# Token blocks of 384 instead of 256 in a pooled-attention and rational-MLP kernel on one Trainium2 core

## The chip, the cores and the metric

The kernel runs on one core of one Trainium2 chip. The metric is the time of one execution on the device in microseconds (us), lower is better. The engines are named as in the profile: PE (TensorE, matmuls; PEld its weight loads), DVE (VectorE), ACT (ScalarE), POOL (GpSimd) and SP (SyncE, which here only issues DMAs). A ratio is time after over time before.

## The reference, cut to what matters

```python
# q, k, v: batch 8, heads 8, seq 576, head_dim 64, float32; pool = 8, so 72 pooled keys
k_p = k.reshape(B, H, 72, 8, D).mean(axis=3)
v_p = v.reshape(B, H, 72, 8, D).mean(axis=3)
scores = D ** -0.5 * q @ k_p.T
attn = softmax(scores) ; attn_out = attn @ v_p
x = attn_out.transpose(0, 2, 1, 3).reshape(4608, 512)     # tokens x d_model
h = x @ w_in                                              # 512 x 2048
P = a0 + a1*h + a2*h^2 + a3*h^3 ; Q = 1 + |b0|*|h| + |b1|*h^2
out = (P / (Q + 1e-6)) @ w_out                            # 2048 x 512, float32
```

## The kernel before

**Tiling.** The 4608 tokens are 18 blocks of `TOK` = 256, `d_ff` is `NU` = 8 units of 256 columns, and one step is one block with one unit. A step has three parts:

- `mm1`: h for 256 columns of `d_ff` by 256 tokens. x and `w_in` are each held as a high and a low part, and three products are summed (high x high, low weight x high, high weight x low): for each of two halves of 128 columns, 3 x 4 matmuls with 256 columns, so 24 into one PSUM bank, tile `ph`.
- `rational` with `quotient`: P/Q of a 128 x 512 tile, in 6 ACT, 5 DVE and 2 POOL instructions (tiles `w`, `r`, `t`, and `rp` in PSUM); the result is split again into `gh` and `gl`.
- `mm2`: 12 matmuls with 512 columns, six for each half of 128 tokens, into two banks `po`, which stay open over all units of a block and are then evicted (`evict`) and stored. The first two blocks are an exception: they run units 0 to 3 first, their x and their partial sums go out to DRAM (`spill`, `parts`), and units 4 to 7 come later (`reload`), so that the weights have time to arrive.

**Attention** (`attend`) makes x of a block. `squares` loads q; `attention` makes, for each tile of 128 tokens, q turned (`qT`), the scores (`ps`), the softmax (tile `e`) and turns that; for blocks from the fifth on q and the softmax are turned in 32 x 32 squares by DVE, and 16 DMAs a block bring the squares from `e` to their places in `am` (high part `hi`, low part `lo`). For the first four blocks PE does the turning (`pq`, `pm`, `pr`). `values` multiplies with the pooled v (tiles `pv`): 16 matmuls a block, or 32 where a batch ends inside the block, since batches have 576 tokens. Six of the 18 blocks have such an end inside. `prep_k` and `prep_v` pool k and v once a batch. The tiles `q`, `am0`, `am1` and `e` have one buffer each, the x tiles `x0` and `x1` two buffers each.

**What sets the order.** Nothing is issued directly. Every call adds an `Op` to a `Plan` with an engine, a cost and a due time (`due(at)`, spaced `SLOW` or `PACE` us a step; single ones are moved by the table `LATER`, which goes by the number of the op). `Plan.solve` then lays the ops out engine by engine by due time, with the pools' buffers as a constraint, and `Plan.issue` emits them in that order, so all instructions carry the one line L309. The PSUM pool `ps` has 8 buffers, one bank each, for `ph`, `rp`, `po`, `ps`, `pv` and the transposes. Where the plan leaves PE free, `issue` puts in matmuls of no use (line L301), which keep PE occupied: into the tile `idle` at the start, and from the first open `po` on, products with zero into an open sum:

```python
elif sums:
    to, one, first = list(sums.values())[-1][:, 0:256].ap(), self.zeros, False
...
while free is not None and to is not None:
    free += 0.12 if free > self.WARM else 0.215
    if free > op.start:
        break
    self.nc.tensor.matmul(to, lhsT=self.filler, rhs=one, start=first, stop=first)
```

Of the kernel before, what the change touches and what calls it, by code (L numbers as in the profile page):

```python
# [72 lines left out]
class Buf:  # L73


    def __init__(self, ring, shape, dtype, name):
        self.ring, self.shape, self.dtype, self.name = ring, shape, dtype, name
        self.writes, self.reads, self.left, self.held, self.it = [], [], 0, False, None
        self.slot, self.users = None, []

# [7 lines left out]
class Ring:  # L88


    def __init__(self, pool, tag, bufs, loose):
        self.pool, self.tag, self.loose = pool, tag, loose
        self.free, self.queue = [(0.0, i) for i in range(bufs)], []


class Op:
    __slots__ = ("eng", "cost", "port", "calls", "deps", "users", "bufs", "due", "wait",
                 "ready", "seq", "bytes", "early", "slack", "start", "end", "done", "lead")


class Plan:
# [3 lines left out]
    HOP = {"sp": 0.035, "pe": 0.035, "pool": 0.08, "dve": 0.035, "act": 0.035}  # L105
# [22 lines left out]
    def __init__(self, nc):  # L128
        self.nc, self.ops, self.rings, self.now, self.slack = nc, [], {}, 0.0, 1.9

# [9 lines left out]
    def add(self, eng, cost, calls, port=False, claims=(), bytes=0, early=34.0, after=()):  # L140
        op = Op()
        op.eng, op.cost, op.port, op.calls, op.bytes = eng, cost, port, calls, bytes
        op.early, op.slack, op.lead = early, self.slack, 0.0
        op.seq, op.due, op.deps, op.users = len(self.ops), self.now, set(), []
# [38 lines left out]
    def solve(self):  # L183
# [17 lines left out]
        while done < len(self.ops):  # L201
            best = None
            for e, cands in engs.items():
                pick = None
                opts = []
                for op in cands:
# [13 lines left out]
                    else:  # L220
                        for r, n in need.values():
                            mine = [b for b in op.bufs if not b.held and b.ring is r]
                            if len(r.free) < n or not r.loose and any(
# [104 lines left out]
def tile_pooled_attention_then_rational_moe(  # L328
# [20 lines left out]
    P = 128  # L349
# [307 lines left out]
    def squares(i):  # L657
# [4 lines left out]
        if i < 4:  # L662
            return qs
# [358 lines left out]
```

## Time and profile before

| | |
|---|---|
| time, median of 3 runs | 899.14 us (899.04 to 899.77) |
| the profiled execution's own time | 898.87 us |
| its span in the profile | 897.2 us |
| granted clock of PE, mean | 0.995 |
| PE busy | 881.1 us, 98% |
| DVE, ACT, POOL busy | 753.1 (84%), 683.2 (76%), 521.3 (58%) |

The profiled execution's time has 1.67 us around the span, and lies 0.27 us under the median of the runs. A matmul's row shows some 275 to 385 ns from its start to its end, but matmuls follow each other much closer, so what one costs is read from the starts of its neighbours in the timeline, not from the mean of its group. In the same way ACT's and DVE's instructions overlap by about 0.1 us.

### The profile page before, as it was taken

What the parts mean: (1) busy time and instruction counts of PE and PEld (TensorE: products, weight loads), DVE (VectorE), ACT (ScalarE), POOL (GpSimd) and SP (SyncE); (2) the same over time, 40 slices, a digit from 0 to 9 for tenths busy, and PEclk for the clock granted to TensorE, in tenths of its full rate; (3) what the DMA queues carried; (4) which work ended last, traced back from release to release, by engine and by line L of the source; (5) the groups of instructions that cost most, each with busy time, mean ns of one, the idle gap of its engine ahead of it and who ended that gap; (6) DMA issues with size and microseconds to landing.
All of it is one profiled execution on the core that took longest, in us unless ns stands there. A gap on an engine that the chain in (4) does not pass through costs nothing.

```text
span 897.2 us, 17205 instructions
## 1 busy us (share of the span) xinstructions
PE 881.1 (98%) x6124; PEld 823.8 (92%) x6124; DVE 753.1 (84%) x1337; ACT 683.2 (76%) x1124; POOL 521.3 (58%) x472
## 2 busy tenths in 40 slices
PE   8799999999999999999999999999999999999998
PEld 8798999899988999999999899999999999999997
DVE  6889997998979869988889699789898977988664
ACT  3799899887676769686877787497868684968774
POOL 5777678886446545455736483467546754545444
PEclk9999999999999999999999999999999999999999
DMA  9996111145133412122613251134222422202000
GB/s 304 300 380 212 32 48 47 51 117 134 44 87 94 107 24 60 30 60 52 131 28 72 54 123 39 31 77 119 59 39 51 96 58 34 51 1 59 2 24 23
DMA packets 185080, 75.31 MB, mean 84 GB/s; under 512 B 162340, under 2 KB 162340, under 8 KB 184996
## 3 DMA queue, kind: packets, MB, share of 16 engines
q1 hardware_dynamic: 184996, 74.23, 32.1%
q8 instruction: 48, 0.79, 0.4%
q14 instruction: 36, 0.29, 0.1%
HBM read 50.59 MB, written 12.58 MB: 70 GB/s over the span
## 4 chain that ended last, share of the span: by engine, by line
PE 81%; ACT 6%; SPq 4%; DMA 3%; DVE 2%; issue 2%; POOL 1%; POOLq 0%; ACTq 0%; DVEq 0%
PE po L309 36%; PE ph L309 36%; PE pv L309 4%; SPq L309 4%; PE ps L309 3%; DMA early<-in_v_dram 2%; ACT rp L309 1%; DVE t L309 1%; ACT r L309 1%; DVE m_wout L309 1%; ACT w L309 1%; ACT t L309 1%; POOL wout L309 1%; DMA ob<-pd 0%; ACT wout L309 0%
## 5 line engine op out<-in xcount | busy, mean ns | idle before, releaser
L309 PEld LDWEIGHTS ph<-x,win 128*128 128x128 f32 x3264 | 455.1, 191 | 32.0 <-issue 0.7
L309 PE MATMUL ph<-x,win 128*128 128x256 f32 x3264 | 464.7, 276 | 0.5 <-ACT x L309 0.4
L309 PE MATMUL po<-wout,gh 128*128 128x512 f32 x1152 | 333.5, 383 | 0.5 <-POOL wout L309 0.3
L309 POOL TENSOR_TENSOR w<-w,r 128x512 f32<-128x512 f32 (+1 forms) x145 | 188.4, 1300 | 216.7 <-ACT r L309 181.3
L309 POOL TENSOR_TENSOR gl<-t,gh 128x512 fp32r<-128x512 f32 (+1 forms) x145 | 189.4, 1307 | 84.3 <-ACT gh L309 70.1
L309 PEld LDWEIGHTS po<-wout,gh 128*128 128x128 f32 x1152 | 187.3, 191 | 10.6 <-ACT gh L309 0.9
L309 PE MATMUL po<-wout,gl 128*128 128x512 f32 x576 | 172.6, 382 | 0.1
L309 DVE SCALAR_TENSOR_TENSOR t<-t,abn,rp 128x512 f32<-128x512 f32 (+1 forms) x145 | 106.8, 736 | 67.2 <-ACT rp L309 65.6
L309 ACT ACTIVATE rp<-w,cbias 128x512 f32<-128x512 f32 (+1 forms) x145 | 99.7, 687 | 55.0 <-POOL w L309 48.6
L309 ACT ACTIVATE w<-ph 128x512 f32<-128x512 f32 (+1 forms) x145 | 85.9, 592 | 50.3 <-PE ph L309 49.7
L309 ACT ACTIVATE r<-w,abn 128x512 f32<-128x512 f32 (+1 forms) x145 | 117.3, 809 | 3.0 <-DVE rp L309 1.6
L309 ACT ACTIVATE t<-ph,abn 128x512 f32<-128x512 f32 (+1 forms) x145 | 111.7, 772 | 10.2 <-PE ph L309 8.6
L309 DVE TENSOR_TENSOR t<-t,ph 128x512 f32<-128x512 f32 (+1 forms) x145 | 97.7, 675 | 18.8 <-ACT t L309 12.8
L309 DVE SCALAR_TENSOR_TENSOR t<-t,abn,ph 128x512 f32<-128x512 f32 (+1 forms) x145 | 106.4, 734 | 1.8
L309 ACT CAST gh<-t 128x512 fp32r<-128x512 f32 (+1 forms) x145 | 88.7, 613 | 21.2 <-PE po L309 17.9
L309 DVE SCALAR_TENSOR_TENSOR t<-rp,t 128x512 f32<-128x512 f32 (+1 forms) x145 | 98.2, 678 | 1.4
L309 DVE SCALAR_TENSOR_TENSOR rp<-w,rp 128x512 f32<-128x512 f32 (+1 forms) x145 | 98.9, 682 | 0.2
L309 PEld LDWEIGHTS po<-wout,gl 128*128 128x128 f32 x576 | 93.8, 191 | 4.9 <-POOL gl L309 0.3
L309 ACT ACTIVATE rp<-rp 128x512 f32<-128x512 f32 (+1 forms) x145 | 84.3, 581 | 2.4
L309 POOL TENSOR_TENSOR e<-e,sm 128x576 f32<-128x576 f32 x36 | 42.9, 1206 | 30.3 <-DVE sm L309 22.2
L309 PE MATMUL pv<-am,vm 128*128 128x256 f32 (+3 forms) x288 | 47.4, 284 | 3.7 <-DVE t L309 3.7
L309 PEld LDWEIGHTS pv<-am,vm 128*128 128x128 f32 x288 | 42.4, 194 | 4.3 <-DVE t L309 4.1
(107 smaller groups left out, 839.6 us busy)
## 6 DMA issues: line engine op xcount, KB each, us to landing
am<-e SPq DMA_DIRECT2D x224, 48.0 KB, 2.1
out_dram<-ob SPq DMA_DIRECT2D x17, 512.0 KB, 3.3
rwin<-in_moe_w_in_dram SPq DMA_DIRECT2D x8, 1024.0 KB, 11.7
rwout<-in_moe_w_out_dram SPq DMA_DIRECT2D x8, 1024.0 KB, 12.9
st_k<-in_k_dram SPq DMA_DIRECT2D x12, 512.0 KB, 4.8
st_v<-in_v_dram SPq DMA_DIRECT2D x12, 512.0 KB, 4.1
q<-in_q_dram SPq DMA_DIRECT2D x144, 32.0 KB, 2.0
st_v<-in_v_dram SPq DMA_DIRECT2D x48, 64.0 KB, 2.2
```

The source lines that it names most:

```text
L309: getattr(engines[op.eng], name)(*map(value, args), **{k: value(v) for k, v in kw.items()})
```

## The change

- **Blocks.** The first three blocks (`SHORT`) keep 256 tokens; from token 768 on there are ten blocks of 384, so 13 in all. `size` and `tok0` give length and first token. Of the 13, block 2 and the long blocks 5, 8 and 11 have a batch's end inside (at their middle).
- **Units.** For a long block a step is 128 columns of `d_ff`, `fs` = (0,) or (1,): `mm1` is 12 matmuls with 384 columns into one bank, `quotient` runs on 128 x 384, `mm2` is 9 matmuls with 512 columns into three banks `po`. A short block's step stays as it was. The last step of all is split in three by tokens, before it was split in two.
- **Order.** All three short blocks run units 0 to 3 first and are spilled, then block 3 runs all units, then the short blocks' units 4 to 7, then blocks 4 to 12.
- **Places.** x is in two tiles by halves of d_model, from a ring of three (`work4`), so that the next block's first half can be written while both halves of the present one are in use. Softmax's parts share places: `hi` and `e` come from one ring with one buffer, `q` and `lo` (`am`) from another.
- **Preparation.** k and v are staged in pieces of 512 columns from three buffers (before: 1024 from two), and k is turned in one go for each batch.
- **Planner.** `kept` holds back banks of the PSUM pool for sums (`keep`, `spare`), POOL's `HOP` is 0.13 (was 0.08), and `LATER`, `HEAD`, `PACE`, `SLOW`, `SLOWS` have new values.

```diff
+    def kept(self, op, bufs):
+        return 0 if bufs[0].sum else max(0, op.keep - self.sums) + op.spare
...
-    TOK = 256
-    NBLK = NT // TOK
+    SHORT, PAIR = 3, True
+    NBLK = SHORT + (NT - SHORT * 256) // 384
...
-    pool("stage", 2)
+    pool("stage", 3)
...
+    pool("work4", 3)
...
-    MM1, MM2 = 111.8, 216.5
+    MM1, MM2 = {256: 111.8, 384: 162.5}, 216.5
...
-        qs = new("work1", "q", [P, NJ, TOK // HB, HB], F32, f"q{i}")
-        if i < 4:
-            return qs
+        shape = [P, NJ, size(i) // HB, HB]
+        if i < SHORT:
+            return new("cpool", "wout6" if i else "win6", shape, F32, f"q{i}")
+        qs = new(*(("cpool", "wout7") if i == SHORT else ("work1", "am")), shape, F32, f"q{i}")
...
-        es = new("work1", "e", [P, NJ + 2, 2, 2 * SP], F32, f"e{i}")
-        for m in range(2):
-            attention(2 * i + m, hi, lo, qs, es)
-        if i >= 4:
+        lo = new("work1", "am", [P, NJ + 2, TOK], F32R, f"am{i}")
+        es = new("work1", "e", [P, NJ + 2, M, 2 * SP], F32, f"e{i}")
...
+            hi = new("work1", "e", [P, NJ + 2, TOK], F32R, f"hi{i}")
...
+        return [(new("work4", "x", [P, 2, 2, size(i)], F32R, f"{name}_{c}"), None)
+                for c in range(2)]
...
-        for f in range(2):
-            for s, (wi, xi) in enumerate(((0, 0), (1, 0), (0, 1))):
+            if len(fs) > 1:
+                groups = [group(*x, range(n)) for x in parts]
+            else:
+                groups = [[y for x in parts for y in group(*x, cs)] for cs in (
+                    range(0, 2), range(2, 4))]
...
-    order += [(i, u) for u0 in (0, NA) for i in (2, 3) for u in range(u0, u0 + NA)]
-    order += [(i, u) for i in range(2) for u in range(NA, NU)]
-    order += [(i, u) for i in range(4, NBLK) for u in range(NU)]
-    HEAD, PACE, SLOW, SLOWS = 15.0, 5.7, 4.5, 2 * NA
+    order += [(2, u) for u in range(NA)]
+    order += [(SHORT, u) for u in range(NU)]
+    order += [(i, u) for i in range(SHORT) for u in range(NA, NU)]
+    order += [(i, u) for i in range(SHORT + 1, NBLK) for u in range(NU)]
...
+        for fs in ((0, 1),) if i < SHORT and PAIR else ((0,), (1,)):
+            steps.append((at, i, u, fs))
+            at += len(fs) * size(i) / 512
+    HEAD, PACE, SLOW, SLOWS = 15.6, 5.8, 5.48, 20
```

Three places show how the order of the instructions moves. In the names below the first number is the block (for `qT` and `ps` the tile of 128 tokens), the next the unit, then the half of the unit; the last number is only a counter.

**PE, in the last block.** Before:

```order
L309 MATMUL ph17_6_10987<-x1_17_10632,win6_1779 128x256 x4
L309 MATMUL po17_0_0_10923<-wout1_763,gh17_1_10905 128x512
L309 MATMUL po17_0_1_10925<-wout1_763,gh17_1_10905 128x512
L309 MATMUL ph17_6_10987<-x0_17_10626,win6_1779 128x256 x4
L309 MATMUL po17_0_0_10923<-wout1_763,gh17_1_10905 128x512
L309 MATMUL po17_0_1_10925<-wout1_763,gh17_1_10905 128x512
```

After, at the same place:

```order
L325 MATMUL ph12_7_0_10774<-x12_1_10204,win7_1708 128x384 x6
L325 MATMUL po12_0_0_10443<-wout4_1912,gh12_4_0_10758 128x512
L325 MATMUL po12_0_1_10446<-wout4_1912,gh12_4_0_10758 128x512
L325 MATMUL po12_0_2_10454<-wout4_1912,gh12_4_0_10758 128x512
L325 MATMUL po12_0_0_10443<-wout4_1912,gh12_4_0_10758 128x512
L325 MATMUL po12_0_1_10446<-wout4_1912,gh12_4_0_10758 128x512
L325 MATMUL po12_0_2_10454<-wout4_1912,gh12_4_0_10758 128x512
L325 MATMUL ph12_7_1_10815<-x12_0_10170,win7_1708 128x384 x6
```

Where four matmuls with 256 columns alternated with two with 512, six with 384 now alternate with six with 512 into three sums.

**PE, ahead of the fourth block's values (`pv3`).** Before:

```order
L309 MATMUL po1_0_1_1152<-wout2_975,gh1_2_1301 128x512
L309 MATMUL ph2_3_1408<-x1_2_1094,win3_731 128x256 x4
L309 MATMUL ph2_3_1408<-x0_2_1087,win3_731 128x256 x8
L309 MATMUL pv3_0_1459<-am0_3_1320,vm01_806 128x256
L309 MATMUL pv3_0_1459<-am0_3_1320,vm11_813 128x256
```

After:

```order
L325 MATMUL po2_0_1_1494<-wout1_850,gl2_1_0_1520 128x512
L317 MATMUL po2_0_1_1494<-zero_87,identr_86 128x256 x21
L325 MATMUL po2_0_0_1492<-wout2_1066,gh2_2_0_1553 128x512
L325 MATMUL po2_0_1_1494<-wout2_1066,gh2_2_0_1553 128x512
L325 MATMUL pv3_0_1582<-hi3_1541,vm01_875 128x384
L325 MATMUL pv3_0_1582<-hi3_1541,vm11_918 128x384
```

A run of 21 zero products now stands there. The program before has 46 filling matmuls, all into `idle`; the program after has 50 into `idle` and 31 zero products, all 31 ahead of the values of block 5.

**SP, around the DMAs that bring the sixth block's softmax to its place (`am1_5`).** Before:

```order
L309 DMA q6_2997<-in_q_dram 32x6x32 x16
L309 DMA q6_2997<-in_q_dram 32x2x32 x6
L309 DMA am1_5_3146<-e5_2966 32x12x32 x4
L309 DMA q6_2997<-in_q_dram 32x2x32
L309 DMA ob1_7_3193<-pd1_1672 128x1024
L309 DMA am1_5_3146<-e5_2966 32x12x32 x4
L309 DMA q6_2997<-in_q_dram 32x2x32 x4
L309 DMA am1_5_3146<-e5_2966 32x12x32 x4
```

After, from the same DMAs of block 5 to those of block 6:

```order
L325 DMA am5_3867<-e5_3592 32x18x32 x16
L325 DMA st_k4_0_4045<-in_k_dram 128x512
L325 DMA st_k4_1_4051<-in_k_dram 128x512
L325 DMA st_k4_2_4055<-in_k_dram 128x512
L325 DMA q6_4171<-in_q_dram 32x12x32 x16
L325 DMA out_0_dram<-ob4_7_0_4383 32x4x512 x2
L325 DMA out_0_dram<-ob4_7_2_4397 32x4x512
L325 DMA am6_4653<-e6_4417 32x18x32 x12
```

Before, the next block's q (`q6`) was loaded ahead of and between the DMAs of `am1_5`. Now all of a block's 16 `am` DMAs stand first, and the next block's q comes behind them, because it uses the place of `am`.

## Rows read from the trace of the kernel before

**Rows 1.** The page's parts 1 and 2: busy time, and the granted clock in 40 slices

```profile
PE 881.1 (98%) x6124; PEld 823.8 (92%) x6124; DVE 753.1 (84%) x1337; ACT 683.2 (76%) x1124; POOL 521.3 (58%) x472
...
PEclk9999999999999999999999999999999999999999
```

**Rows 2.** Windows: stretch, length; busy PE, PEld, DVE, ACT, POOL; clock, DMA share, GB/s

```profile
60.00:80.00 20.00, 19.73 (x150) 17.78 (x150) 18.86 (x37) 19.55 (x33) 15.67 (x11) 1.00 1.03 380
91.00:109.00 18.00, 18.00 (x134) 16.85 (x133) 17.01 (x33) 13.87 (x28) 13.16 (x12) 1.00 0.20 32
300.00:800.00 500.00, 498.61 (x3506) 469.29 (x3505) 429.10 (x775) 375.88 (x621) 270.47 (x230) 1.00 0.28 62
```

**Rows 3.** Waits of PE: who waited, for whom; us in total, times, longest

```profile
PE pv L309 <- DVE t L309: 3.7, 2, 2.3
```

**Rows 4.** Timeline of PE, last block: start, length, operation, form, count

```profile
837.74 0.60 PE L309 MATMUL po<-wout,gh 128*128 128x512 f32 x2
838.17 0.61 PE L309 MATMUL ph<-x,win 128*128 128x256 f32 x4
...
862.33 0.60 PE L309 MATMUL po<-wout,gl 128*128 128x512 f32 x2
...
881.21 1.03 PE L309 MATMUL po<-wout,gh 128*128 128x512 f32 x4
...
888.98 1.03 PE L309 MATMUL po<-wout,gh 128*128 128x512 f32 x4
```

**Rows 5.** Timeline of PE around values (pv) with and without a batch's end

```profile
225.32 0.34 PE L309 MATMUL pv<-am,vm 128*128 128x128 f32 x2
...
551.70 0.31 PE L309 MATMUL pv<-am,vm 128*128 128x64 f32 x2
...
554.96 0.62 PE L309 MATMUL po<-wout,gl 128*128 128x512 f32 x2
...
646.98 0.33 PE L309 MATMUL pv<-am,vm 128*128 128x128 f32 x2
...
834.96 0.41 PE L309 MATMUL pv<-am,vm 128*128 128x256 f32 x2
...
836.86 0.60 PE L309 MATMUL po<-wout,gh 128*128 128x512 f32 x2
```

**Rows 6.** Timeline of PE around transposes (pq) and scores (ps)

```profile
61.35 0.60 PE L309 MATMUL pq<-identr,q 128*128 128x128 f32 x4
61.70 0.68 PE L309 MATMUL po<-wout,gh 128*128 128x512 f32 x2
...
63.10 1.22 PE L309 MATMUL ps<-kpT,qT 128*128 128x144 f32 x8
64.06 0.70 PE L309 MATMUL ph<-x,win 128*128 128x256 f32 x4
```

**Rows 7.** Groups by form: busy, mean ns of one; idle before, releasers

```profile
L309 ACT ACTIVATE r<-w,abn 128x512 f32<-128x512 f32 x143 | 116.1, 812 | 3.0 <-DVE rp L309 1.6 <-POOL gl L309 0.7
L309 DVE SCALAR_TENSOR_TENSOR t<-rp,t 128x512 f32<-128x512 f32 x143 | 97.4, 682 | 1.3
...
L309 ACT ACTIVATE r<-w,abn 128x256 f32<-128x256 f32 x2 | 1.2, 596 | 0.0
...
L309 DVE SCALAR_TENSOR_TENSOR t<-rp,t 128x256 f32<-128x256 f32 x2 | 0.8, 420 | 0.0
```

**Rows 8.** Timeline of PE and of SP's queue around one block's softmax

```profile
605.21 0.66 PE L309 MATMUL ps<-kpT,qT 128*128 128x144 f32 x4
...
613.70 9.00 SPq L309 DMA_DIRECT2D q<-in_q_dram  x16
...
627.06 11.47 SPq L309 DMA_DIRECT2D am<-e  x16
```

More of the change, by code (lines that the diff above doesn't have):

```diff
@@ L138, in tile, with add @@
         return Lazy(b)
-    def add(self, eng, cost, calls, port=False, claims=(), bytes=0, early=34.0, after=()):
+    def add(self, eng, cost, calls, port=False, claims=(), bytes=0, early=40.0, after=()):
         op = Op()
@@ L531, in prep_k @@
         pl = bank(f"pl{n}", [P, P])
-        for c0, c1, np in ((0, 2, P), (2, 4, P), (4, 5, H * SP - 4 * P)):
+        every = new("work1", "ks", [P, 5, 2, D], F32, f"ks{n}")
+        pieces = ((0, 2, P), (2, 4, P)) if n < 2 else tuple((c, c + 1, P) for c in range(4))
+        for c0, c1, np in (*pieces, (4, 5, H * SP - 4 * P)):
             nc_ = c1 - c0
@@ L753, in attention, with whole, values @@
                 in1=lo[P // 2:, NJ:, col].bitcast(F32), op=ALU.subtract)
[L755 to L759 removed]
+    def whole(i):
+        return len(segs(tok0(i), size(i))) == 1
+    def values(i, high, lo):
+        n, xs = size(i), x_of(i, f"x{i}")
+        step = 512 // n
+        for j0 in range(0, NJ, step):
+            pv = bank(f"pv{i}_{j0}", [P, step, n])
@@ L781, in attend, with x_at @@
+    def x_at(xs, s, j):
+        j0 = j if isinstance(j, int) else j.start
+        tile, c = xs[j0 // 2]
+        j = j % 2 if isinstance(j, int) else slice(j0 % 2, j0 % 2 + j.stop - j0)
+        idx = slice(None), s, j, slice(None)
+        return tile, idx if c is None else (idx[0], c, *idx[1:])
+    prepared, shared = set(), {}
     def attend(i):
-        for _, _, n in segs(i * TOK, TOK):
+        for _, _, n in segs(tok0(i), size(i)):
             if n not in prepared:
@@ L919, in mm2 @@
-        if i < 2 and not u0:
-            parts[i] = new("hbm", f"pd{i}", [P, 2, DM], F32, f"pd{i}")
-            dma(512, parts[i], ob)
-        else:
-            dma(512, rows_of(i).rearrange("m j b x -> j b m x"), ob)
-    def rows_of(i):
-        return out[i * TOK:(i + 1) * TOK, :].rearrange("(b m j) x -> m j b x", b=2, m=2)
+        if i >= SHORT and (begins or ends):
+            for m in range(M):
+                for n in range(len(terms)):
+                    products(n, (m,))
+        else:
+            for n in range(len(terms)):
+                end = products(n, range(M))
@@ new lines, in mm2 @@
+        if not ends:
+            return
+        if i < SHORT:
+            ob = new("dec", "m", [P, 2, DM], F32, f"ob{i}_{u}")
+            if u0:
+                dma(512, ob, parts.pop(i), after=(end,))
+            for m in range(2):
+                po = pos[i][m]
+                if u0:
+                    dve(DM).scalar_tensor_tensor(out=ob[:, m, :], in0=po, scalar=1.0 / WS,
+                                                 in1=ob[:, m, :], op0=ALU.mult, op1=ALU.add)
+                else:
+                    evict(m, ob[:, m, :], po)
+            if not u0:
+                parts[i] = new("hbm", f"pd{i}", [P, 2, DM], F32, f"pd{i}")
+                dma(512, parts[i], ob)
+            else:
+                dma(512, rows_of(i).rearrange("m s u v x -> s u v m x" if whole(i) else
+                                              "m j b x -> j b m x"), ob)
+            return
```

297 lines of the change are left out of this document (169 added, 128 removed), and 21 rows, old and new, of the table LATER.

## Prediction, made before the changed kernel ran

> **What bounds the kernel now.** I read the page's busy shares first, then windows, then PE's waits, then PE's timeline. PE is busy 98% of the span at the full granted clock, that is 2.4 GHz; DVE follows with 84%, ACT with 76% [rows 1]. From 300 to 800 us PE is busy 498.6 of 500 us, DVE 86% and ACT 75% of them [rows 2]. In all that time PE waits visibly in two places, 3.7 us together, both for values whose operands DVE had not finished [rows 3]. But "busy" of a pipelined engine says little about whether it could go faster, so I price its instructions by the distance of their starts. In the last block, 28 repeats of four 256-column and two 512-column matmuls take 862.33 - 837.74 = 24.59 us; later 36 matmuls with 512 columns alone take 888.98 - 881.21 = 7.77 us, 215.8 ns each [rows 4]. So 112 matmuls with 256 columns take 24.59 - 56 x 0.2158 = 12.5 us, 111.7 ns each. Values take 836.86 - 834.96 = 1.90 us in a whole block and 554.96 - 551.70 = 3.26 us in one with a batch's end inside [rows 5]; a tile's scores 0.96 us, four transposes 0.35 us [rows 6].
>
> The test of these prices: from block 4's values to block 13's, 9 blocks pass in 646.98 - 225.32 = 421.7 us, 46.85 a block [rows 5]. Priced: 192 x 0.1117 + 96 x 0.2158 = 42.17, scores 1.92, values (6 x 1.90 + 3 x 3.26) / 9 = 2.35, together 46.4. The 0.4 that is left is the 3.7 us of waits over nine blocks. So PE's instruction stream is the bound, and the change is worth what it takes from that stream, as long as nobody makes PE wait.
>
> **The change part by part**, against the span of 897.2 us.
>
> - *mm1.* 15 of the 18 blocks had 15 x 192 = 2880 matmuls with 256 columns, 321.7 us. Ten long blocks have 1920 with 384. No row shows this form. The neighbours bound it: at 2.4 GHz 256 columns take 106.7 ns and the row has 5.0 more, 512 take 213.3 and the row has 2.5 more, so 384 take 160 + 2.5 to 160 + 5.0, 162.5 to 165.0. I take the middle, 163.8, since it lies as near to one row as to the other: 314.5 us, **-7.2** (-9.7 to -4.9). No matmul of `mm2` goes away: 1728 of them before and after.
> - By the Trainium skill, "TensorE: Matmul & The Clock Gate", section "Back-to-back issue gap", a matmul at the fast clock follows another after its columns at 2.4 GHz plus 2.5 ns. The trace agrees at 512 columns (215.8) and not at 256 (109.2 by the page, 111.7 here); by it the sum would be 2.5 us lower.
> - *Values.* A whole long block takes 16 matmuls of 0.119 + 0.052 us (half of what 512 columns cost above 256), 2.73 us. A split one has 32 with 192 columns, between the mean of the split row (0.102) and the 256-column one (0.119), so 3.3 to 3.8; I take 3.5. Before: 12 x 1.90 + 6 x 3.26 = 42.4. After: 2 x 1.90 + 3.26 + 7 x 2.73 + 3 x 3.5 = 36.7. **-5.6** (-6.4 to -4.8). Most of this is that a 384-token grid has only four blocks with a batch's end inside.
> - *Transposes.* Six tiles instead of eight are turned by PE, 20 transposes fewer: **-1.8** on PE. DVE gets two tiles' squares more, and the softmax of block 3 takes 16 DMAs in that stage; this lies beside PE's work in a stretch where DVE had 6% left (60 to 80 us) [rows 2], so it costs nothing as long as the rival below on ACT and DVE doesn't hold.
> - *Filling matmuls.* The program has 31 zero products and four fillers more. Each stands for time in which PE waits by the order itself, at 111.7 ns **+3.9**. They could take the place of waits that were there already (then 0), but in 60 to 80 us PE was idle only 0.27 us [rows 2], so I take all of it.
> - *Waits at values.* Two waits in the 17 changes of block cost 3.7 us [rows 3]. With 12 changes left, 2.6: **-1.1** (from none, -3.7, to twice as much as now, +3.7).
> - *Loads.* Block 3's q now comes in 128-byte pieces in the first stage, 0.79 MB. In 91 to 109 us, when mostly such loads ran, the queues moved 32 GB/s at 20% [rows 2], so 160 GB/s at full use: 4.9 us of a resource that is full from 60 to 80 us, and the weights behind it land later by as much. Three short blocks of work on units 0 to 3 and block 3 lie ahead of unit 4, where before four short blocks did; that hides it, and I cost it at 0, at most +4.9. The k and v pieces are twice as many DMAs on SP and small POOL instructions; POOL is at 58% and not on the path.
>
> Sum: -7.2 - 5.6 - 1.8 + 3.9 - 1.1 = -11.8, a span of 885.4. The profiled execution has 1.67 us around its span, and is 0.27 under the median: **887.3 us**, -1.3%. For a whole long block this is 16 x (12 x 0.1638 + 9 x 0.2158) + 3 x 0.96 + 2.73 = 68.2 us, where one and a half blocks took 70.3.
>
> **Rivals.**
>
> - *ACT and DVE take it back.* The pointwise work is cut in 184 sets instead of 144. Twice the 256 form less the 512 form is what one instruction more costs at most: ACT 0.38 us, DVE 0.16 us [rows 7] (at most, because neighbours overlap). A long block has 16 sets where 12 were, so ACT gets 4 x 6 x 0.38 = 9.1 us more, on 35.2 x 1.5 = 52.8 (75% of 46.85 is 35.2), 61.9 of 68.2; DVE 60.3 + 4 x 5 x 0.16 = 63.5 of 68.2. So neither bounds a late block, and for that I count against this rival. For it: from 60 to 80 us ACT was busy 19.55 of 20 [rows 2], and block 3 now runs there in halves of units. If its 9.1 us of extra ACT time lie on the path, the time is 896.4. The Trainium skill, "Perfetto Trace Analysis", section "Optimizing Scalar/DVE Operations", speaks against such small instructions: it gives each a fixed cost, some 93 ns on ACT from SBUF, and prefers larger ones where the engine is saturated; by its figure 240 more ACT instructions are an estimated 22 us, far less than by rows 7.
> - *The softmax's shared places make a chain (slower).* q can't be loaded while the last block's `am` is in use, `hi` can't be written before `e` is read. So a long block's attention is one chain: 16 q loads 9.0 us; from the first scores to the first `am` DMA 627.06 - 605.21 = 21.9 for two tiles, so 32.8 for three; from there to the values 646.98 - 627.06 = 19.9; values 2.7 [rows 5, 8]. That is 64.4, under the 68.2 of a block. A split block has 32 q loads, 73.4 against 69: 4.4 us over at three blocks, 900.5. Each further us in the chain costs 3, and from 3.8 more on every block pays; 1.5 us more give 905. Against it: these intervals were not pressed, the next block's q was already under way in them, the first half of a split block's q suffices for its first tile, and no zero product stands behind the values of block 5, so the order itself foresees no such wait.
> - *The wider matmul saves nothing.* If 384 columns cost 1.5 times what 256 do (167.6 ns), `mm1` stays at 321.7, and the time is 894.5. The 512 row, well under twice the 256 row, speaks against it.
>
> **How the numbers follow.** Chances: forecast 0.64, in its own range 878 to 895 (the low ends of `mm1`, values, fillers and waits add up to -9.9; the high ends without the loads to +6.8, the loads in part); still lower 0.06; ACT and DVE 0.12; no saving by width 0.04; the chain 0.10; something else at the early stage that eats all 0.04. The range 878 to 898 takes in all but the chain, the unnamed case and the tail below. A measurement of this kernel can tell some 0.2% from no change, so "same" is 897.3 to 900.9. Faster: 0.64 + 0.06 + 0.12 + 0.04 = 0.86. The chain gives 0.02 of same and 0.08 of slower, the unnamed case 0.03 and 0.01: same 0.05, slower 0.09.
>
> **What would show it.** Right: in the late blocks six 384-column matmuls start 0.98 us before the next group; values of block to block lie some 68 us apart; PE's visible waits stay at a few us; the span before the values of block 5 is no better than the prices say, the gain of some 2 us a long block comes evenly behind it. Wrong: PE rows that wait for ACT (`gh`) or POOL (`gl`) in runs of long blocks; waits of PE for `hi` or `am` at blocks 5, 8 and 11; PE below 19 of 20 us in the stage from 40 to 130 us, where I took the first stage to be no worse but for its fillers.

## The result and the profile after

The changed kernel takes 885.11 us (median of four runs, 883.58 to 885.76), the kernel before beside it 899.45 us (899.04 to 899.94): a ratio of 0.984, 95% interval 0.982 to 0.986, 14.3 us less. The forecast was 887.3. The profiled execution is the fastest of the four, 883.58 us with a span of 881.9, so in the traces the difference of the spans is 15.3 us, one more than between the medians.

The page of the changed kernel, part 1 (busy time, share of the span, instructions) and the granted clock of part 2, against [rows 1]:

```profile
PE 865.2 (98%) x5067; PEld 805.5 (91%) x5067; DVE 769.7 (87%) x1585; ACT 725.2 (82%) x1373; POOL 549.9 (62%) x614
...
PEclk9999999999999999999999999999999999999999
```

PE has 1057 matmuls fewer and 15.9 us less busy time. DVE, ACT and POOL have 17, 42 and 29 us more: their work is nearly the same (DVE turns two tiles more), in more and smaller instructions.

Windows (columns as in [rows 2]), first of the changed kernel, then of the kernel before where [rows 2] have no such stretch:

```profile
0.00:130.00 130.00, 118.94 (x818) 109.97 (x819) 115.36 (x214) 102.85 (x168) 90.67 (x106) 0.97 0.78 239
300.00:800.00 500.00, 499.64 (x2818) 467.50 (x2817) 450.36 (x972) 415.19 (x817) 293.35 (x330) 1.00 0.30 64
34.00:41.00 7.00, 3.18 (x27) 2.77 (x25) 6.73 (x16) 6.97 (x12) 4.68 (x4) 0.92 0.71 136
41.00:48.00 7.00, 6.77 (x41) 5.94 (x42) 6.14 (x12) 5.37 (x13) 4.55 (x3) 0.59 1.01 369
```

```profile
0.00:130.00 130.00, 122.54 (x870) 113.39 (x871) 111.44 (x203) 105.16 (x180) 92.28 (x113) 0.99 0.68 220
34.00:41.00 7.00, 5.85 (x48) 5.04 (x46) 5.88 (x14) 5.13 (x16) 4.78 (x5) 1.00 1.15 292
```

From 300 to 800 us PE is now busy 499.6 of 500, with DVE at 90% (86% before) and ACT at 83% (75%). In the first 130 us PE does less than before: 118.9 us against 122.5, and some of that is zero products.

PE's largest waits, against [rows 3] (us in total, times, longest):

```profile
PE pm L325 <- POOL e L325: 3.2, 1, 3.2
PE idle L325 <- DVE identr L1089: 2.1, 1, 2.1
PE po L325 <- ACT gh L325: 1.7, 2, 0.9
PE pq L325 <- DMA q<-in_q_dram: 1.5, 2, 0.8
...
PE pv L325 <- DVE am L325: 0.7, 1, 0.7
...
PE pv L325 <- DVE t L325: 0.3, 1, 0.3
```

All but the last lie in the first stage. The waits at values of [rows 3], 3.7 us, are down to 0.3.

**The new price.** PE's timeline in the last block, as in [rows 4] (start, length, operation, form, count):

```profile
830.18 1.14 PE L325 MATMUL ph<-x,win 128*128 128x384 f32 x6
831.15 0.81 PE L325 MATMUL po<-wout,gl 128*128 128x512 f32 x3
...
862.29 0.81 PE L325 MATMUL po<-wout,gl 128*128 128x512 f32 x3
```

Six matmuls with 384 columns take 0.97 us to the next group. From 831.15 to 862.29 the stretch of twelve 384-column and nine 512-column matmuls repeats eight times, 31.14 us. With 215.8 ns for 512 columns [rows 4], 96 matmuls take 31.14 - 72 x 0.2158 = 15.60 us: 162.5 ns each, the low end of the forecast's 162.5 to 165.0. This is also what the rule gives that the prediction cites from the Trainium skill ("TensorE: Matmul & The Clock Gate", section "Back-to-back issue gap"). There the Trainium skill calls it the gap of a single matmul by itself, and gives some 131 ns at 512 columns for a stream of weight loads and matmuls. This trace is such a stream and agrees with the rule at 512 and 384 columns (215.8 and 162.5), not with the 131; at 256 columns the rule is low here (109.2 against 111.7).

**The new block.** PE's timeline at the first matmul of values of block 3 (and the first group behind them), 4, 5 (a batch's end inside, and the group behind them) and 12, against [rows 5]:

```profile
122.03 0.49 PE L325 MATMUL pv<-hi,vm 128*128 128x384 f32 x2
...
124.63 0.59 PE L325 MATMUL po<-wout,gh 128*128 128x512 f32 x2
...
254.14 0.49 PE L325 MATMUL pv<-hi,vm 128*128 128x384 f32 x2
...
323.55 0.36 PE L325 MATMUL pv<-hi,vm 128*128 128x192 f32 x2
...
326.91 0.83 PE L325 MATMUL po<-wout,gh 128*128 128x512 f32 x3
...
800.98 0.49 PE L325 MATMUL pv<-hi,vm 128*128 128x384 f32 x2
```

Eight long blocks pass in 800.98 - 254.14 = 546.84 us, 68.36 each; one and a half blocks before took 70.28. So a long block saves 1.92 us. Values take 2.60 us in a whole long block and 3.36 in a split one. From these rows, mm1 saves 192 x (1.5 x 0.1117 - 0.1625) = 0.97 us a block, values 0.64 (1.5 x 2.35 before, 23.1 / 8 = 2.89 now), and 0.31 is what is left over prices: 0.62 in one and a half blocks before, 0.31 now. The 0.31 that is left now isn't waits that the profile shows, since PE waits 0.3 us in all from 300 to 800 us; the prices themselves are good to some 0.3 us a block.

Ten long blocks at 1.92 would be 19.2 us. The spans differ by 15.3. So the rest, the first stage above all, lost 3.9 us, and this loss, together with how near the next bound is, was what the experiments were for.

### The profile page after: what moved, and what is told of

Its sections match the earlier page's. It is cut to its first block, busy times and chain, and to the rows that moved or that the text cites. A ratio compares the mean times of both kernels' runs of the same rounds, so it can differ in the third digit from the quotient of the medians.

```text
span 881.9 us, 15828 instructions
## 1 busy us (share of the span) xinstructions
PE 865.2 (98%) x5067; PEld 805.5 (91%) x5067; DVE 769.7 (87%) x1585; ACT 725.2 (82%) x1373; POOL 549.9 (62%) x614
## 4 chain that ended last, share of the span: by engine, by line
PE 82%; ACT 7%; DVE 5%; DMA 3%; POOL 2%; issue 1%; SPq 1%; POOLq 0%; DVEq 0%; ACTq 0%
PE ph L325 36%; PE po L325 36%; PE ps L325 4%; PE pv L325 3%; DMA q<-in_q_dram 2%; DVE t L325 2%; ACT rp L325 1%; SPq L325 1%; ACT t L325 1%; PE pvs L325 1%; ACT hi L325 1%; ACT r L325 1%; ACT w L325 1%; DVE e L325 1%; ACT gh L325 1%
## 5 line engine op out<-in xcount | busy, mean ns | idle before, releaser
L325 PE MATMUL ph<-x,win 128*128 128x384 f32 (+1 forms) x2208 | 380.1, 321 | 1.1 <-POOL win L325 0.6
L325 POOL TENSOR_TENSOR w<-w,r 128x384 f32<-128x384 f32 (+2 forms) x186 | 196.2, 1056 | 148.4 <-ACT r L325 136.8
L325 POOL TENSOR_TENSOR gl<-t,gh 128x384 fp32r<-128x384 f32 (+2 forms) x186 | 201.3, 1083 | 127.2 <-ACT gh L325 95.2
L325 DVE SCALAR_TENSOR_TENSOR t<-t,abn,rp 128x384 f32<-128x384 f32 (+2 forms) x186 | 114.7, 618 | 58.4 <-ACT rp L325 57.2
L325 ACT ACTIVATE t<-ph,abn 128x384 f32<-128x384 f32 (+2 forms) x186 | 125.8, 678 | 35.8 <-DVE rp L325 13.9
L325 ACT ACTIVATE r<-w,abn 128x384 f32<-128x384 f32 (+2 forms) x186 | 133.1, 715 | 9.0 <-POOL gl L325 4.1
L325 ACT ACTIVATE rp<-w,cbias 128x384 f32<-128x384 f32 (+2 forms) x186 | 110.7, 595 | 30.6 <-POOL w L325 25.8
L325 DVE SCALAR_TENSOR_TENSOR t<-t,abn,ph 128x384 f32<-128x384 f32 (+2 forms) x186 | 114.5, 616 | 1.2
L325 DVE SCALAR_TENSOR_TENSOR t<-rp,t 128x384 f32<-128x384 f32 (+2 forms) x186 | 104.0, 559 | 1.9
L325 DVE SCALAR_TENSOR_TENSOR rp<-w,rp 128x384 f32<-128x384 f32 (+2 forms) x186 | 105.0, 565 | 0.0
```

What stands on the lines that cost most here:

```text
L325: getattr(engines[op.eng], name)(*map(value, args), **{k: value(v) for k, v in kw.items()})
```

## Experiments

Ratios are to the kernel before, run beside; the changed kernel stands at 0.984.

| Run | Time, us | Ratio, 95% interval |
|---|---|---|
| `p_width` | 930.69 | one run, no interval |
| `e_nozero` | 887.26 | 0.9856 (0.9840 to 0.9871) |
| `e_due_none_after` | 892.34 | 0.9916 (0.9902 to 0.9929) |
| `e_due_none_before` | 906.55 | 1.0068 (1.0053 to 1.0083) |
| `e_q3_runs` | 884.34 | 0.9827 (0.9807 to 0.9847) |
| `e_256` | 933.04 | 1.0367 (1.0348 to 1.0386) |
| `e_256_apart` | 925.28 | 1.0296 (1.0268 to 1.0323) |
| `e_11of12` | 882.32 | 0.9798 (0.9777 to 0.9819) |
| `e_11_nomul` | 871.71 | 0.9689 (0.9667 to 0.9711) |
| `e_11_noexp` | 876.61 | 0.9747 (0.9726 to 0.9767) |
| `e_act_b3` | 891.64 | 0.9903 (0.9886 to 0.9919) |
| `e_b3_noexp` | 884.84 | 0.9840 (0.9819 to 0.9862) |

### The price of a matmul by its width

```diff
...
+        for n in (512, 448, 384, 320, 256, 192, 128, 64):
+            for _ in range(40):
+                self.nc.tensor.matmul(to[:, 0:n], lhsT=self.filler, rhs=self.last.ap()[:, 0, 0:n],
+                                      start=True, stop=True)
```

> The changed kernel with 320 matmuls added behind its last product: 40 each with 512, 448, 384, 320, 256, 192, 128 and 64 columns, every one with a weight load of its own as in the kernel; they read the weights and write a bank that nobody uses. What one matmul costs by its width, on its own. My prediction's middle: 163.8 ns at 384 columns, on a line between 111.7 (256) and 215.8 (512). Theory from the changed kernel's trace: 162.5 at 384, and the 5 ns more at 256 than its columns at 2.4 GHz (106.7) are the first sign of a floor that does not depend on the columns: 320 then comes to 135.8 (columns plus 2.5), and 192, 128 and 64 stay between 100 and 112. Rival: a fixed price of 2.5 to 5 ns at every width: 192 would be 83 to 85, 128 some 57, 64 some 30. Time of the whole: some 45 us above the changed kernel by the theory, 38 by the rival.

The run took 930.69 us, 45.6 more than the changed kernel, where the theory had some 45 and the rival 38. Its groups by form (busy time of the forty, mean ns of one):

```profile
L331 PE MATMUL probe<-wout,identr 128*128 128x512 f32 x40 | 9.3, 392 | 0.0
...
L331 PE MATMUL probe<-wout,identr 128*128 128x384 f32 x40 | 7.1, 336 | 0.0
L331 PE MATMUL probe<-wout,identr 128*128 128x320 f32 x40 | 6.0, 308 | 0.0
...
L331 PE MATMUL probe<-wout,identr 128*128 128x256 f32 x40 | 4.9, 279 | 0.0
L331 PE MATMUL probe<-wout,identr 128*128 128x192 f32 x40 | 4.6, 274 | 0.0
L331 PE MATMUL probe<-wout,identr 128*128 128x128 f32 x40 | 4.6, 274 | 0.0
```

Forty overlap, so the distance of two starts is (busy - one) / 39: 228 ns at 512 columns, 173 at 384, 146 at 320, 118 at 256, and 111 at both 192 and 128. (The 64 columns ran partly at 1.2 GHz at the very end and are left out.) A fixed surcharge to the columns, the rival, is out: below 256 columns the price stops falling. What the floor is made of, no run was made to show. By the Trainium skill, "TensorE: Matmul & The Clock Gate", section "LDWEIGHTS (loading the stationary operand)", loading weights takes their columns at 1.2 GHz, an estimated 106.7 ns for 128 columns. Each matmul here has its own load of 128 columns, and the floor of 111 ns lies 4 ns above this estimate. Rows of the kernel before point the same way: at values with 128 columns (block 4) one matmul of four loads 64 columns of weights instead of 128, and six such groups of four take

```profile
226.00 0.23 PE L309 MATMUL pv<-am,vr 128*64 128x128 f32 x1
...
228.37 0.22 PE L309 MATMUL pv<-am,vr 128*64 128x128 f32 x1
```

2.37 us, 395 ns a group. Four at the floor would take 444 ns, so the one with half the load costs some 62 ns (an estimate that gives the other three 111).

The absolute level was not settled in this way: the train costs 7 to 13 ns more at 256 to 512 columns than the same widths in the kernel (111.7, 162.5 and 215.8). Where that comes from stays open; the train writes one bank anew each time, the kernel mostly adds up. In the train 256 columns still lie some 7 ns above the floor, in the kernel at it. For the kernel its own rows count. What carries over is the shape, a floor below some 256 columns and a price by columns above it: 256 columns sit at the floor's edge and 384 well above it, and that is the saving.

### The zero products

```diff
-                elif sums:
-                    to, one, first = list(sums.values())[-1][:, 0:256].ap(), self.zeros, False
```

> The changed kernel without its 31 zero products; the order of everything else is the same. My prediction charged them, with four fillers, +3.9 us. Theory now: they stand where PE waits for gh of block 2 and for the like (behind the 21 of them at 118.16 us PE still waits 0.82 us), so time doesn't change: 885.1, within 0.7. Rival, the prediction's own step: they are instructions like others, and without them the time is 3.5 us lower, 881.6.

Without them the time did not fall to the rival's 881.6; the ratio is 0.0018 higher (1.6 us), with intervals that overlap. The median lies 2.1 us above the theory's 885.1, more than the 0.7 that it allowed. The timelines of PE behind block 2's last `gl` products, of the changed kernel and of this run:

```profile
117.73 0.59 PE L325 MATMUL po<-wout,gl 128*128 128x512 f32 x2
118.16 2.51 PE L317 MATMUL po<-zero,identr 128*128 128x256 f32 x21
121.49 0.70 PE L325 MATMUL po<-wout,gh 128*128 128x512 f32 x2 [0.82 <-ACT gh L325]
```

```profile
118.56 0.59 PE L323 MATMUL po<-wout,gl 128*128 128x512 f32 x2
122.28 0.70 PE L323 MATMUL po<-wout,gh 128*128 128x512 f32 x2 [3.13 <-ACT gh L323]
```

The wait for `gh` is there either way: 2.5 us of zero products and 0.82 us of waiting, or 3.13 us of waiting. And the bare wait costs something else. Windows of this run and of the changed kernel:

```profile
118.00:125.00 7.00, 3.87 (x17) 3.22 (x16) 6.31 (x8) 6.93 (x10) 3.00 (x3) 0.88 0.18 67
125.00:130.00 5.00, 5.00 (x25) 4.66 (x24) 3.34 (x7) 3.60 (x6) 4.33 (x3) 0.82 0.19 32
```

```profile
118.00:125.00 7.00, 6.18 (x43) 5.78 (x42) 6.91 (x9) 6.93 (x10) 3.26 (x3) 1.00 0.08 33
125.00:130.00 5.00, 5.00 (x32) 4.87 (x31) 3.67 (x7) 4.17 (x8) 3.92 (x2) 1.00 0.49 79
```

Behind the bare wait the granted clock falls from 2.4 to 1.2 GHz for a while: 7 x 0.12 + 5 x 0.18 = 1.7 us of full-speed time is gone, which fits the 1.6 us, though the intervals don't tell these from none. With zero products the clock stays up: from 118 to 130 us it is 1.00 in the traces of the changed kernel and of all six runs below that keep these products and its table. So they cost nothing, and the wait that they fill is a real one, of ACT. The expectation calls "instructions like others" the prediction's own step; the prediction's words were that each "stands for time in which PE waits by the order itself", and that is what the run shows.

### The due times

```diff
-    LATER = { 83: -4, 85: -17, 95: 2, ...
+    LATER = {}
```

The second run empties the table of the kernel before in the same way.

> The changed kernel with its table of due times (LATER) empty, all else as it is, so that the planner's own order stands. Theory: the gain comes from the wider blocks, and the due times trim waits that are a few us in either program: 887 to 893 (PE's stream by prices 848.2 against 846.5, the rest waits). Together with the kernel before, its table emptied too, the difference stays at -14, within 4. Rival: the table anew is a large part of the gain; then this run is at 895 or more while the other hardly moves.

> The kernel before with its table of due times empty. Theory: 902 to 908 (PE's stream by prices 861.8 against 859.4, the rest waits), so that the difference to the changed kernel without a table is again about -14. Rival (the gain is the new table): 899 to 901.

892.34 and 906.55: each kernel loses some 7 us without its table, and the ratio between the two is 0.9916 / 1.0068 = 0.985, against 0.984 with tables. The gain is not in the new table.

### Block 3's q in small pieces

```diff
+                    if i == SHORT:
+                        dma((r1 - r0) / 8, qs[g * HB:(g + 1) * HB, j, r0 // HB:r1 // HB, :],
+                            q[n, 2 * j + hh, s0 + d0 // HB * 192:s0 + d0 // HB * 192 + 192].rearrange(
+                                "(s r) d -> s (r d)", s=HB).rearrange("s (b x) -> s b x", x=HB), run=128)
+                        continue
```

> The changed kernel with block 3's q read in runs of 1536 bytes instead of 128: the same 16 transfers of the same size at the same places in the order, but other elements of q land in the tile, so the outputs of tokens 768 to 1151 are not the reference's. My prediction costed the small pieces at 0, at most 4.9 us (0.79 MB at 160 GB/s). From 0 to 130 us PE was busy 118.9 us in the changed kernel and 122.5 before, with 3.5 us of zero products in it, so about 7 us are lost there. Theory: the loss is a chain on DVE, ACT and POOL (the one wait of 3.2 us is for POOL's e of block 1), not the loads; 885.1, within 1. Rival: the small pieces hold up the weights behind them; 2 to 5 us faster, 880 to 883.

884.34 us, ratio 0.983: no difference that the intervals tell. The cost of 0 for these loads holds, within some 2 us. The wait for block 1's `e` has the same length here (3.2 us), so it doesn't hang on these loads. In the changed kernel, around that wait (34 to 41 us), ACT is busy 6.97 of 7 us and DVE 6.73 while PE is busy 3.18 (window above); before it was 5.13, 5.88 and 5.85. That these two make `e` late is the reading; no run took work from them there.

### Blocks of 256 tokens in the changed program

```diff
-    NBLK = SHORT + (NT - SHORT * 256) // 384
+    NBLK = NT // 256
...
-        return 256 if i < SHORT else 384
+        return 256
...
-        for fs in ((0, 1),) if i < SHORT and PAIR else ((0,), (1,)):
+        for fs in ((0, 1),):
...
-        plan.keep = 3 if i >= SHORT else 2 if again else 0
+        plan.keep = 2 if i >= SHORT or again else 0
```

> The changed kernel with blocks of 256 tokens throughout, in pairs of units, all else as changed (x in three pieces, the shared places, the first stage with block 3 in it, the planner's rule that keeps banks back, set to two sums), and the table of due times empty, since its numbers no longer fit. To be held against the changed kernel without a table (892.3). Theory: the length of the blocks is the gain. PE's stream by prices is 872.0 against 848.2: mm1 and values are worth 15.2 of that, and the order itself foresees 14 us of waits, filled with zero products, where blocks of 46.4 us are too short for the attention's chain through the shared places: 907 to 916. Rival: pieces, places and pairs make the gain and the length little: below 899.

It took 933.04 us, 17 above the theory's range and 40.7 above the long blocks without a table. A second run gives `q` and `hi` places of their own and keeps no banks back:

```diff
-            hi = new("work1", "e", [P, NJ + 2, TOK], F32R, f"hi{i}")
+            hi = new("work1", "hi", [P, NJ + 2, TOK], F32R, f"hi{i}")
...
-        qs = new(*(("cpool", "wout7") if i == SHORT else ("work1", "am")), shape, F32, f"q{i}")
+        qs = new(*(("cpool", "wout7") if i == SHORT else ("work1", "q")), shape, F32, f"q{i}")
...
-        return 0 if bufs[0].sum else max(0, op.keep - self.sums) + op.spare
+        return 0
```

> The run with 256-token blocks throughout (933.0), with places of their own for q and hi again and no banks kept back. Its table of due times is empty as well. My rival B was a chain through the shared places; at 384 tokens no wait of it was seen, at 256 the blocks of the run lay 49.7 us apart where the kernel before has 46.85. Theory: the shared places make that, since the chain (64.4 us for three tiles, by my prediction's intervals some 50 for two) fits in 68 us and not in 46.5: blocks go back to 46.5 to 47, and the time to 905 to 915 (against 892.3 for long blocks without a table). Rival: the places cost nothing, and pairs and pieces do: 925 or more.

925.28 us: the theory's 905 to 915 missed, and the rival's bound of 925 just met. PE's timeline at the first matmul of values of block 4 and of block 17, with shared places, then with places apart:

```profile
235.33 0.34 PE L312 MATMUL pv<-hi,vm 128*128 128x128 f32 x2
...
881.25 0.38 PE L312 MATMUL pv<-hi,vm 128*128 128x256 f32 x2
```

```profile
240.24 0.34 PE L312 MATMUL pv<-hi,vm 128*128 128x128 f32 x2
...
860.80 0.38 PE L312 MATMUL pv<-hi,vm 128*128 128x256 f32 x2
```

The values of these blocks lie 49.7 us apart with shared places and 47.7 with places apart; the kernel before has 46.85. But with shared places block 17's values start only 50.2 us before the end of the span (931.4), with places apart 62.8 (span 923.6), and before 62.2, so this distance takes some lateness of values for pace. From block 4's values to the end the three have 696.1, 683.4 and 671.9 us: shared places with the kept banks are 12.7 of the 24.2 us that these fourteen blocks are slower, some 0.9 of 1.7 us a block. PE's largest wait is one that the softmax's chain (rival B) names, but in both runs, first with shared places, then with places apart:

```profile
PE pv L312 <- DVE am L312: 6.7, 6, 2.5
```

```profile
PE pv L312 <- DVE am L312: 4.5, 4, 2.2
```

So that wait isn't the mark of the shared places, and since the second run also took back the kept banks, the two do not show what a chain through the places costs. In a block of 68 us there is no sign of it: 0.7 us of waits for `am` in the whole changed kernel, and those at block 0. The other half, and what lies outside these blocks, were not taken apart: pairs, three pieces of x and the new first stage are all in it. The missing table alone isn't it, as the kernel before stands at 906.55 us without its own. The runs say that the changed program needs the long block, not what each of its parts costs.

### How near the next bound is

One of twelve products of each `mm1` group in the long blocks is left out, with the order of all that remains unchanged:

```diff
                            s == 0 and c == 0, s == 2 and c == n - 1) for c in cs
+                        if tok == 256 or (s, c) != (1, n - 1)]
...
-                end = pe(MM1[tok] * len(calls), calls, after=end),
+                end = pe(MM1[tok] * (4 if len(fs) > 1 else 6), calls, after=end),
```

> The changed kernel with one of the twelve products of each mm1 group in long blocks left out (160 matmuls with 384 columns, at the same places in the order), so its outputs aren't the reference's. How far the next bound is. Theory: PE's stream alone bounds, ACT (83% of 300 to 800 us) and DVE (90%) have room for 2.6 us less per block: 160 x 0.1625 = 26.0 us less, at least 22 of them seen: 859 to 863. Rival (ACT and DVE bind already, so that PE merely looks full): 870 or more.

The theory (859 to 863) fell, and the rival's 870 or more was met. PE had 26 us less to do, and the time fell by 2.8 us (3.6 by the ratios). The window of the late blocks and PE's timeline at values of block 4 and block 12:

```profile
300.00:800.00 500.00, 488.56 (x2703) 447.94 (x2702) 452.45 (x974) 415.59 (x818) 295.25 (x332) 1.00 0.30 64
```

```profile
255.35 0.49 PE L325 MATMUL pv<-hi,vm 128*128 128x384 f32 x2
...
801.82 0.49 PE L325 MATMUL pv<-hi,vm 128*128 128x384 f32 x2
```

546.47 us for eight blocks, where the changed kernel has 546.84. The blocks run no faster although each holds 2.6 us less for PE; DVE and ACT are as busy as before (452.5 and 415.6). So PE's stream and something else turn at the same pace, within 0.05 us a block. PE's stream fills the late blocks of the changed kernel to 0.31 us, but taking more from it makes them no shorter.

Which of the others it is, two further runs ask; both start from this one:

```diff
+        drop[0] = tok > 256
...
-        dve(W).tensor_tensor(out=t, in0=t, in1=h, op=ALU.mult)
+        op = dve(W).tensor_tensor(out=t, in0=t, in1=h, op=ALU.mult)
+        if drop[0]:
+            op.calls = []
```

> The run with one of twelve mm1 products left out (882.3), and in the long blocks DVE's product of t with ph left out too (160 instructions of 0.546 us, 87 us of DVE; PE's order unchanged). Outputs aren't the reference's. That run gave 3 us where PE had 26 less to do, so something else turns at almost the same pace. Theory: it is DVE (90% busy from 300 to 800 us, and the order of its queue fixed): with DVE lighter PE's 26 us show, 859 to 864. Rival: ACT, or the chain through all engines; then 875 or more.

```diff
+        drop[0] = tok > 256
...
-        act(W).activation(rp, rp, AF.Exp, scale=-1.0)
+        op = act(W).activation(rp, rp, AF.Exp, scale=-1.0)
+        if drop[0]:
+            op.calls = []
```

> The run with one of twelve mm1 products left out (882.3), and in the long blocks ACT's second pass on rp (Exp) left out too: 160 instructions of 0.48 us, 77 us of ACT. Outputs aren't the reference's. If DVE alone is what turns beside PE, this gives little: 876 to 882. If ACT is it: 859 to 864. If it is the chain from ph to gl through ACT, DVE and POOL, both this run and its neighbour without DVE's product gain, by some 10 to 20 us each.

871.71 and 876.61 us: with 160 DVE instructions left out (87 us by their rows, 67 of DVE's busy time) another 10.6 us show, with 160 of ACT (77 us by their rows, 63 of its busy time) another 5.7. The windows, DVE's run first:

```profile
300.00:800.00 500.00, 494.02 (x2750) 456.01 (x2749) 410.42 (x867) 424.31 (x835) 298.63 (x335) 1.00 0.29 64
```

```profile
300.00:800.00 500.00, 489.69 (x2722) 451.39 (x2721) 456.19 (x977) 375.77 (x709) 296.32 (x332) 1.00 0.29 64
```

With DVE at 82% and with ACT at 75% PE is still not full. From block 4's values to block 12's a block takes 67.17 us (254.79 to 792.16) and 67.70 us (253.85 to 795.48), where PE's stream asks for some 65.8, 2.6 less than 68.36. None of the cases written down fits both numbers. DVE alone asks for 859 to 864 in the first run, ACT alone for the same in the second, and the chain through ACT, DVE and POOL for some 10 to 20 us in both, where the second gains 5.7; 876.61 lies in the range written for DVE alone. What stands next to PE is mostly DVE: in the run with one product left out PE is idle 11.4 us from 300 to 800 us (0.4 in the changed kernel), and of its waits there 8.6 us end with DVE's work and 1.6 with ACT's, in many places of at most 1.1 us. The largest group is at values:

```profile
PE pv L325 <- DVE am L325: 2.1, 3, 0.9
```

So DVE's queue is the likely next bound, with something else some 1.1 us a block behind it. What that is stays open: ACT, the waits of these engines for one another in queues of fixed order, or the softmax's chain. Neither a run with the order planned anew for the shorter PE work nor one with places apart at 384 tokens was made.

### ACT in block 3

```diff
+        twice[0] = i == SHORT
...
-        act(W, claims=early).activation(w, h, AF.Abs, scale=1.0 / WS)
+        op = act(W, claims=early).activation(w, h, AF.Abs, scale=1.0 / WS)
+        if twice[0]:
+            op.calls = op.calls * 2
```

> The changed kernel with the first of ACT's instructions on ph (the absolute value) done twice in block 3 alone: 16 more of some 0.49 us, 7.8 us of ACT, between about 75 and 130 us, where block 3 meets the first stage. My rival A priced ACT's extra instructions of block 3 at 9.1 us if they lay on the path. Theory: ACT is the one that is waited for from 100 to 130 us (28.97 of 30 us busy; behind the 21 zero products at 118.16 PE waits for gh) but not from 60 to 100, so a part shows: 2 to 5 us, 887 to 890. Rival A as a whole: 893. No part on the path: 885.

891.64 us: 6.5 us of the 7.8 added show, more than the theory's 2 to 5. The second run takes ACT work away at the same place (`Exp`, by the edit shown above, in block 3 only, with all products of PE):

> The changed kernel with ACT's second pass on rp (Exp) left out in block 3 alone: 16 instructions of 0.48 us, 7.7 us of ACT between about 75 and 180 us. Outputs of tokens 768 to 1151 aren't the reference's. Twice the absolute value there cost 6.5 us of the 7.8 added. Theory: ACT is on the path where block 3 meets the first stage, as the changed kernel stands; the waits that it causes there are the 3.3 us before block 2's gh and the small ones from 130 to 200 us (0.75 us): 881 to 883. Rival: ACT was just not on the path, and only work added puts it there: 885, within 0.7.

884.84 us, the same as the changed kernel: the theory (881 to 883) missed and the rival (885) was met. Windows of the run with more ACT work, then with less:

```profile
130.00:200.00 70.00, 66.02 (x370) 60.54 (x369) 51.99 (x91) 66.38 (x122) 56.65 (x66) 0.98 0.20 58
...
146.00:150.00 4.00, 3.72 (x10) 3.08 (x11) 3.63 (x7) 3.76 (x8) 2.68 (x5) 0.59 0.33 90
```

```profile
100.00:130.00 30.00, 29.22 (x182) 27.02 (x181) 27.46 (x39) 28.95 (x44) 24.24 (x14) 1.00 0.56 133
130.00:200.00 70.00, 69.83 (x413) 65.15 (x412) 57.19 (x98) 60.11 (x102) 64.17 (x71) 1.00 0.24 68
```

Block 3's values start at 122.03 us, and its pointwise work lies behind 130 us for the most part, later than both expectations had it: without `Exp` ACT's busy time there falls from 64.8 to 60.1 us, and PE, already full, rises by 0.6. From 100 to 130 us, where ACT is full (28.95 of 30), nothing changes, since the sets that it works on there are the short blocks'. So ACT is at its edge in block 3, but not over it: work added shows, work taken away doesn't. Of the 6.5 us some 1.6 are the clock, which fell to 1.2 GHz with a wait of 1.4 us that ends at 146.28 (4 us at 0.59).

## Why the prediction was right, and where it was not

The direction, the size and the mechanism were right: 885.1 against 887.3, PE full in the late blocks, and values 68.36 us apart, a mean over five whole and three split blocks, for which the prediction's prices give 68.4 (its 68.2 for a whole block adds up to 68.1, and a split one to 68.9). Term by term, on spans:

- **mm1: mis-sized.** -7.2 forecast, 1920 x 0.1625 - 321.7 = -9.7 measured. The step "I take the middle, 163.8, since it lies as near to one row as to the other" failed. The surcharges of the two rows were not two points of one line: the 256 row sits at the edge of a floor, the 512 row on the slope, and 384 belongs to the slope. `p_width` shows the bend.
- **Values: a little low.** -5.6 forecast. Measured 2 x 1.90, a split short one of 3.4 (in two halves, 1.70 us from 69.65 and 1.72 from 82.17), 7 x 2.60 and 3 x 3.36: 35.5 us instead of 42.4, -6.9 (the whole short blocks at the price of [rows 5]). A 384-column matmul of values costs 162.5 ns as in `mm1`, not 171.
- **Transposes:** 20 fewer, as forecast; at the forecast's price -1.8.
- **Filling matmuls: right in kind.** +3.9 was charged for the waits that they stand for. `e_nozero` shows that they cost nothing by themselves: their time is a wait that exists without them. But the reason for charging all of it ("in 60 to 80 us PE was idle only 0.27 us") looked at the wrong stretch; 21 of the 31 stand at 118 us, where ACT's `gh` of block 2 is late. And they mark only part of the new waits (see the first stage below).
- **Waits at values:** -1.1 forecast. What a long block has over its prices fell by 0.31 us, some 3 us over ten blocks. So "The 0.4 that is left is the 3.7 us of waits over nine blocks" held only within the 0.3 us a block to which the prices are good. One part of the old cost was not in the forecast's prices: with the wait of 2.3 us of [rows 3], at 270 us, the clock fell (last section).
- **Loads:** 0, as forecast (`e_q3_runs`).
- **First stage: seen in part.** "I took the first stage to be no worse but for its fillers." It is worse. The measured difference of -15.3 less the three terms of the stream (-9.7 - 6.9 - 1.8 = -18.4) leaves +3.1 for all waits, with the products that fill them; the late blocks gained about 3 of waits, so the first stage's cost about 6 more (3.9 net, since some 2.3 of the transposes' and values' saving lies there too). PE's work there agrees: 118.9 less 2.5 us of zero products is 6.1 under 122.5. Two places are named above: 3.2 us for block 1's `e` at 37.8 us, with DVE and ACT full, and 3.3 us for block 2's `gh` at 118 us. Behind the first of them the clock fell too (last section), which the kernel before doesn't show there. How the 6 us divide among these, and what the waits of the kernel before in this stage take off them (2.8 us for q is the largest), no run shows. That the forecast had +3.9 - 1.1 = +2.8 for the sum, against +3.1, is luck: it had some 2 us too little lost in the first stage and some 2 us too little gained in the late blocks.

On spans the gain was 3.5 us larger than forecast: 2.5 more from `mm1`, 1.3 more from values, 0.3 less from waits and fillers. The median lies 1.5 us above the profiled execution, where 0.3 had been allowed for, and so 2.2 us are left between 887.3 and 885.1. One sum of the range is off: with waits from -1.1 to +3.7 the high ends add up to +7.9, not +6.8, which the range up to 895 still all but covers.

Of the rivals, **the wider matmul saves nothing** is refuted by the row of 162.5 ns. **The softmax's chain** did not occur: no wait for `hi` or `am` at blocks 5, 8 and 11. Its sum was too long for the split blocks at least, where 73.4 us against 69 would have shown; the reasons given against it (the intervals were not pressed, half of a split block's q suffices at first) fit that, but were not tested. `e_256` and `e_256_apart` don't show the chain by itself, since the wait for `am` is there in both. **ACT and DVE take it back** did not decide either, but it was judged by a wrong measure. For it the prediction said that block 3 now runs from 60 to 80 us; block 3's values start only at 122. Its bounds for a late block (ACT 61.9, DVE 63.5 of 68.2 us) were, if anything, too high; measured are 83% and 90%, that is 56.8 and 61.6. And yet "neither bounds a late block" left no more room: with PE lighter the block stays at 68.3 us, with DVE lighter too it takes 67.2. So busy shares of 83% and 90% left next to no room. That the waits between these engines are part of their pace is the likely reason, not a shown one. The forecast's mechanism, that the change is worth what it takes from PE's stream, held for this change and was used up by it.

The due-time table, which the prediction left out of its sum, was rightly left out: the ratio is the same with and without.

## What to carry to other kernels

Price a width that no row shows from the rows on its own side of the bend: in this kernel, where each matmul loads its own weights, the price is flat up to some width and then goes with the columns, and the gain of a wider form is how far the narrow one sits under that bend. Fillers in a schedule mark waits that the schedule foresees; charge the wait, and ask who causes it. A busy share under 100% is not yet room: whether a second engine or a chain turns at the same pace is shown by making the first bound lighter and looking whether the block gets shorter.

## What the runs showed of the hardware that was not expected

- With a weight load for each, matmuls of 128 and 192 columns both took 111 ns; 256 columns 118 in the same train. In the kernel 256 take 111.7, 384 162.5 and 512 215.8 ns.
- A wait of PE can cost more than its length, when the granted clock falls to 1.2 GHz with it. With the 3.19 us wait of the changed kernel, from 37.8 us, it is 0.92 from 34 to 41 us and 0.59 from 41 to 48: 3.4 us of full-speed time, some of it in the wait itself (in four other runs with that wait the clock from 41 to 48 is 0.58 to 0.77, so this varies). The kernel before has it too, with the 2.28 us wait that ends at 270.39:

```profile
262.00:272.00 10.00, 7.56 (x51) 6.89 (x50) 7.27 (x11) 8.28 (x14) 3.79 (x3) 0.95 0.10 17
272.00:280.00 8.00, 8.00 (x51) 7.19 (x52) 6.47 (x15) 4.09 (x8) 2.72 (x3) 0.85 0.51 141
```

Here 10 x 0.05 + 8 x 0.15 = 1.7 us are gone, a cost of [rows 3] that the prediction did not count. Matmuls that add zero, put into the wait at 118 us, went with a clock of 2.4 GHz throughout, and without them it fell to 1.2.
